# Batch 0's kv sum turned instead of direct, and three moves in the opening of an attention and MLP kernel

## The chip, the cores and the metric

The kernel runs on one NeuronCore of a Trainium2 chip. The metric is the device time of one execution in microseconds. The engines of the core are called by the names of the profile: PE is TensorE (matrix products; PEld is its loading of weights), DVE is VectorE, ACT is ScalarE, POOL is GpSimd, SP is SyncE, which here only issues transfers (DMA). Each engine works through its own queue in order, and engines wait for each other by semaphores.

## The reference, cut to what matters

A polynomial-sketch attention feeds a two-layer network with an exact GELU.

```python
batch, n_heads, seq, head_dim = (4, 4, 1088, 32); r = 8
def phi(x):
    a = einsum('rd,bhsd->bhsr', S1, x)
    b = einsum('rd,bhsd->bhsr', S2, x)
    return einsum('bhsi,bhsj->bhsij', a, b)          # flattened to 64 features
q_p, k_p = phi(q), phi(k)
kv  = einsum('bhsf,bhsd->bhfd', k_p, v)
z   = sum(k_p, axis=2)
num = einsum('bhsf,bhfd->bhsd', q_p, kv)
den = einsum('bhsf,bhf->bhs', q_p, z)[..., None] + 1e-6
x   = (num / den), heads side by side: (4352, 128)
out = gelu_exact(x @ w_in) @ w_out                    # w_in 128 x 2048, w_out 2048 x 128
```

q, k and v are float32. S1, S2, w_in and w_out arrive as float64, so the kernel rounds them to float32 itself.

## The kernel before, in words

**Chunks.** The 4352 tokens are worked in chunks of 512 tokens, two to a batch, and one last chunk that holds the 64 tokens left over of each batch. Chunk n is turned into features, divided, brought into the layout xT (128 features of x by 512 tokens) and then passed through the network: for each of 16 column tiles of w_in a hidden product (function `hidden`, line 683), GELU on ACT (690), and the product with w_out. For most of chunk time the second product runs in a scheme that takes seven block products where eight would be needed (`two_products`, 768); the first eight column tiles of chunks 0 and 1 use plain products (`project`, 819).

**The order of the work** is written out by hand. Lines 851 to 918 are the opening: the sketches, batch 0's keys and values, the features of chunk 0, the rounding of the first weights. After it a list of steps runs, one per chunk and column tile; other work is put at steps by `at(step, function)`. At the end of the program (1122 to 1128) every instruction is tied to the one before it on its engine, so each engine keeps the order of the text.

**Batch 0's kv.** Keys are transposed on PE (333), multiplied with the sketches (373), and turned to features by ACT and DVE or POOL (386 to 390). `kv_first` (411 to 418) then sums over tokens: 128 tokens at a time, the 64 features of a head are the stationary operand and 32 values with a one beside them (33 columns, which gives z as well) are the moving operand. Two heads use the two column halves of PE. `kv_first_rem` (420 to 424) adds the left-over tokens. The result stands as features by values, the layout which the numerators want, and one ACT copy (888) brings it from PSUM into `kz[0]`. Later batches do it the other way round: `kv_sum` (428) has v stationary and features moving, `take_kv` copies, and `turn_kv` turns the result on PE.

**Numerators and dividing.** `numerators_by_token` (635) multiplies chunk 0's expanded query features by `kz[0]`; `divide` (650 denominators, 651 reciprocals, 656 products) runs on DVE; `turn_half` (664, 665) transposes each half of 256 tokens and copies it to xT, half 0 by ACT and half 1 by DVE. `first_hidden` (698) starts the network on the halves.

**Expanding queries.** `expand_products` (534) makes both sketched factors of a chunk's query features, A in the first half of the columns and B in the second, in two pairs of PSUM banks; `expand_copy` (541, ACT) takes A to SBUF, `expand_multiply` (546, DVE) multiplies with B from PSUM. For chunk 1 the queries are transposed on PE by `query_turn(1)` (515, through 333), and the copy of that result is kept back and run at 895.

**Rounding weights.** `Rounding` splits the float64 words: ACT scales the low words (260), DVE cuts out exponent field (268) and mantissa field (273), ACT makes exponents (279), DVE adds the mantissa (287) and sign (292), and DVE or POOL forms the product (297). One piece of w_out gets its mantissa from ACT and POOL (284, 285). w_in has pieces of 256, 256, 512, 512 and 512 columns, w_out the same in rows.

**Loads.** SP issues them in one queue. The load of w_out's first two pieces is held back by two small POOL memsets (180) which stand behind POOL's product for w_in piece 0; every further load is queued behind them.

**Spread sketches.** `spread_sketches` (466 to 478) forms, with eight POOL instructions, copies of the sketches for the later batches. It is put at step 11; the matrix products that use it come first at 44.8 us.

## Time and profile before

| what | us |
|---|---|
| median of 3 runs | 264.18 (263.84 to 264.23) |
| the profiled execution | 264.42 |
| its span, first to last instruction | 262.6 |
| PE busy in the span | 257.3 (98%) |
| DVE busy | 151.3 (58%) |
| ACT busy | 116.7 (44%) |
| POOL busy | 163.8 (62%) |
| mean granted PE clock | 0.999 |

How to read a profile line: start and duration in us (or, in groups, the busy sum), the engine, the line of the kernel, the operation, what it writes and reads ("out<-in", partitions x elements), how many; in square brackets the idle time of the engine just before, and what ended it. In the chain of waits each row is a piece of the chain that ended last: start, length, engine, what it wrote, line. Matmuls are pipelined and their ends are modelled, and releasers are inferred from semaphores.

### The profile page before, as it was taken

What the parts mean: (1) busy time and instruction counts of PE and PEld (TensorE: products, weight loads), DVE (VectorE), ACT (ScalarE), POOL (GpSimd) and SP (SyncE); (2) the same over time, 40 slices, a digit from 0 to 9 for tenths busy, and PEclk for the clock granted to TensorE, in tenths of its full rate; (3) what the DMA queues carried; (4) which work ended last, traced back from release to release, by engine and by line L of the source; (5) the groups of instructions that cost most, each with busy time, mean ns of one, the idle gap of its engine ahead of it and who ended that gap; (6) DMA issues with size and microseconds to landing.
All of it is one profiled execution on the core that took longest, in us unless ns stands there. A gap on an engine that the chain in (4) does not pass through costs nothing.

```text
span 262.6 us, 5749 instructions
## 1 busy us (share of the span) xinstructions
PE 257.3 (98%) x2329; PEld 132.3 (50%) x2329; DVE 151.3 (58%) x307; ACT 116.7 (44%) x227; POOL 163.8 (62%) x173
## 2 busy tenths in 40 slices
PE   8999999999999999999999999999999999999994
PEld 6844444344454554444444455444444444445794
DVE  2885878969697996591267957450647042600240
ACT  3674777442635334543434334533362335433441
POOL 3403006899968676687767766867778676877200
PEclk9999999999999999999999999999999999999999
DMA  7479648730001101002000010011000100010020
GB/s 207 131 211 365 147 102 209 213 78 13 0 2 17 25 4 28 13 2 40 2 0 2 0 29 15 2 24 16 2 0 13 31 4 0 12 31 0 2 40 20
DMA packets 29530, 13.48 MB, mean 51 GB/s; under 512 B 21824, under 2 KB 27712, under 8 KB 29504
## 3 DMA queue, kind: packets, MB, share of 16 engines
q1 hardware_dynamic: 29472, 13.12, 20.2%
q8 instruction: 18, 0.29, 0.5%
q14 instruction: 8, 0.07, 0.1%
q10 hardware_dynamic: 32, 0.00, 0.0%
HBM read 10.88 MB, written 2.23 MB: 50 GB/s over the span
## 4 chain that ended last, share of the span: by engine, by line
PE 93%; DVE 3%; ACT 1%; issue 1%; POOL 1%; DVEq 0%
PE h_ps L683 43%; PE o_ps L768 33%; PE o_ps L819 5%; PE w_ps L816 3%; PE w_ps L617 2%; PE w_ps L428 1%; PE w_ps L849 1%; PE w_ps L568 1%; PE o_ps L417 1%; PE h_ps L333 1%; PE w_ps L935 1%; DVE q_pT L546 0%; PE w_ps L534 0%; DVE x_tok L656 0%; DVE w_out L297 0%
## 5 line engine op out<-in xcount | busy, mean ns | idle before, releaser
L683 PE MATMUL h_ps<-xT,w_in 128*64 128x512 f32 (+3 forms) x516 | 138.7, 577 | 0.0
L690 ACT ACTIVATE block<-h_ps 128x512 f32<-128x512 f32 (+1 forms) x128 | 73.0, 570 | 121.6 <-PE h_ps L683 115.1
L768 PE MATMUL o_ps<-block,w_out 128*64 128x256 f32 x224 | 57.8, 380 | 0.3 <-DVE sums L789 0.3
L683 PEld LDWEIGHTS h_ps<-xT,w_in 128*64 128x64 f32 (+1 forms) x516 | 42.0, 143 | 30.1 <-issue 11.4
L733 POOL TENSOR_TENSOR bits_low<-block 128x512 f32<-128x512 f32 x28 | 35.6, 1273 | 28.6 <-ACT block L690 28.6
L768 PEld LDWEIGHTS o_ps<-block,w_out 128*64 128x64 f32 x224 | 30.2, 137 | 38.8 <-issue 25.8
L734 POOL TENSOR_TENSOR bits_a<-block 128x512 f32<-128x512 f32 x28 | 35.7, 1277 | 14.0 <-ACT block L690 14.0
L735 POOL TENSOR_TENSOR bits_e<-bits_a,block 128x512 f32<-128x512 f32 x28 | 36.3, 1297 | 2.2
L736 POOL TENSOR_TENSOR bits_m<-block,bits_e 128x512 f32<-128x512 f32 x28 | 35.8, 1280 | 2.2
L784 DVE TENSOR_TENSOR sums<-o_ps,sums 64x512 f32<-64x512 f32 x8 | 5.5, 682 | 41.3 <-ACT sums L781 23.6
L768 PE MATMUL o_ps<-bits_low,small 128*64 128x256 f32 x112 | 29.2, 383 | 0.0
L768 PE MATMUL o_ps<-block,small 128*64 128x256 f32 x112 | 29.1, 383 | 0.0
L768 PE MATMUL o_ps<-bits_a,small 128*64 128x256 f32 x112 | 29.0, 382 | 0.0
L768 PE MATMUL o_ps<-bits_m,w_out 128*64 128x256 f32 x112 | 28.8, 380 | 0.0
L580 DVE STREAM_TRANSPOSE w_ps<-w_ps 128x512 f32<-128x512 f32 (+1 forms) x7 | 4.8, 691 | 38.5 <-PE w_ps L568 38.5
L768 PEld LDWEIGHTS o_ps<-block,small 128*64 128x64 f32 x112 | 14.7, 137 | 18.4 <-issue 10.0
L768 PE MATMUL o_ps<-bits_e,small 128*64 128x256 f32 x112 | 17.2, 385 | 0.0
L819 PE MATMUL o_ps<-g,w_out 128*128 128x512 f32 x32 | 16.4, 600 | 0.5 <-DVE w_out L297 0.5
L768 PEld LDWEIGHTS o_ps<-bits_m,w_out 128*64 128x64 f32 x112 | 15.4, 137 | 0.0
L768 PEld LDWEIGHTS o_ps<-bits_a,small 128*64 128x64 f32 x112 | 14.9, 137 | 0.0
L768 PEld LDWEIGHTS o_ps<-bits_low,small 128*64 128x64 f32 x112 | 14.7, 137 | 0.0
L690 ACT ACTIVATE g<-h_ps 128x512 f32<-128x512 f32 x16 | 9.5, 594 | 7.7 <-PE h_ps L683 7.1
(181 smaller groups left out, 297.2 us busy)
## 6 DMA issues: line engine op xcount, KB each, us to landing
out_dram<-oT SPq DMA_DIRECT2D x26, 64.0 KB, 2.2
block<-in_moe_w_in_dram SPq DMA_DIRECT2D x3, 512.0 KB, 7.1
block<-in_moe_w_out_dram SPq DMA_DIRECT2D x3, 512.0 KB, 13.0
k<-in_k_dram SPq DMA_DIRECT2D x12, 128.0 KB, 3.0
v<-in_v_dram SPq DMA_DIRECT2D x12, 128.0 KB, 3.3
q<-in_q_dram SPq DMA_DIRECT2D x24, 64.0 KB, 2.2
k<-in_k_dram SPq DMA_DIRECT2D x2, 256.0 KB, 2.8
q<-in_q_dram SPq DMA_DIRECT2D x2, 256.0 KB, 4.2
```

What stands on the lines that cost most here:

```text
L580: dve.transpose(out=tok, in_=ps[:, :, :H2])
L617: pe.matmul(banks[h * D:(h + 1) * D, s, i * N:(i + 1) * N], lhsT=(kz[b] if b else kz_first)[rows, h * D:(h + 1) * D], rhs=f[rows, h // 2, ...
L683: pe.matmul(ps[rows, :W], lhsT=w[:, rows], rhs=xT[n][:, :W], start=True, stop=True)
L690: act.activation(out=g_of[n, fi][:, :W], in_=ps[:, :W], func=ACT.Gelu)
L733: pool.tensor_sub(out=s[3], in0=a11, in1=a21)
L734: pool.tensor_add(out=s[1], in0=a21, in1=a22)
L735: pool.tensor_sub(out=s[2], in0=s[1], in1=a11)
L736: pool.tensor_sub(out=s[4], in0=a12, in1=s[2])
L768: pe.matmul(acc[n][bank][half * 64:(half + 1) * 64, col:col + HW], lhsT=fixed, rhs=moving, start=opens and e == 0 and name in "4715", stop ...
L784: dve.tensor_add(out=C[lo, 1], in0=a1[lo], in1=C[lo, 0])
L816: pe.matmul(o_of[n][i][:, :128], lhsT=g[:, i * 128:(i + 1) * 128], rhs=w_tile(w_out_sb, fi), start=first, stop=final)
L819: pe.matmul(o_of[n], lhsT=w_tile(w_out_sb, fi), rhs=g, start=first, stop=final)
```

## The change

- `kv_first` and `kv_first_rem` swap their operands: values with the one (33 columns) are stationary, the 64 features move. The sum stands as values by features in `kv_bank[:, :128]`.
- `take_kv_first` (new) copies it to SBUF with two ACT copies, one per head pair; `turn_kv_first` (new) turns it on PE with four products by the identity into `kv_bank[:, 128:256]`; the old copy to `kz[0]` reads from there. The turn is issued in the middle of `query_turn(1)`, between the second and the third transpose.
- The exponents of w_in piece 0 (279, ACT) move from ahead of that copy to behind it.
- Of chunk 0's two query multiplies (546, DVE), the second moves behind the field cuts of w_in piece 0.
- `expand_products` can do one half: chunk 1's A half stays where it was, `expand_copy(1, 0)` moves up behind the dividing, and the B half comes between the two `turn_half` calls.
- `spread_sketches` moves from step 11 into the opening, behind `widen_v_rem(0)`.

```diff
     def kv_first(ps, r, tokens=range(J)):
...
             for c in range(NP):
-                pe.matmul(ps[c * F:(c + 1) * F, r * 2 * D:r * 2 * D + C], lhsT=flat(k_p[0, r][:, t, c * 4 + ch * 2 + one]),
-                          rhs=v_aug[r][:, c, i, :C], start=(r == 0 and i == 0), stop=False, skip_group_check=True)
+                pe.matmul(ps[c * F:c * F + C, r * F:(r + 1) * F], lhsT=v_aug[r][:, c, i, :C],
+                          rhs=flat(k_p[0, r][:, t, c * 4 + ch * 2 + one]), start=(r == 0 and i == 0), stop=False,
+                          skip_group_check=True)
...
+    def take_kv_first(ps):
+        kv_T[0] = big.tile([128, 128], FP, name="kv_T_first")
+        for c in range(NP):
+            rows = slice(c * F, c * F + C)
+            act.copy(out=kv_T[0][rows], in_=ps[rows, :128])
+
+    def turn_kv_first(ps):
+        for c in range(NP):
+            rows = slice(c * F, c * F + C)
+            for r in range(2):
+                pe.matmul(ps[c * F:(c + 1) * F, r * F:r * F + C], lhsT=kv_T[0][rows, r * F:(r + 1) * F], rhs=ident[rows, rows],
+                          start=True, stop=True)
...
-    def expand_products(n):
+    def expand_products(n, parts=range(2)):
...
-        for i in range(2):
-            B_of[n, i] = work_banks()
-        for s in range(2):
+        if 0 in parts:
+            qp[n] = att.tile([128, 2, CW], FP, name="q_pT")
+            for i in range(2):
+                B_of[n, i] = work_banks()
+        for s in parts:
...
     widen_v_rem(0)
+    spread_sketches()
     expand_products(0)
-    for i in range(2):
-        query_features(0, i)
+    expand_copy(0, 0)
+    expand_copy(0, 1)
+    expand_multiply(0, 0)
...
     w_in[0].fields()
+    expand_multiply(0, 1)
+    take_kv_first(kv_bank)
+    late = []
+    query_turn(1, lambda **a: late.append(a), lambda: turn_kv_first(kv_bank[:, 128:256]))
+    kz_of, kv_of = (x.rearrange("f (r x) -> f r x", r=2)[:, :, :C] for x in (kz[0], kv_bank[:, 128:256]))
+    act.copy(out=kz_of, in_=kv_of)
     w_in[0].exponents()
-    late = []
-    query_turn(1, lambda **a: late.append(a))
-    kz_of, kv_of = (x.rearrange("f (r x) -> f r x", r=2)[:, :, :C] for x in (kz[0], kv_bank[:, :128]))
-    act.copy(out=kz_of, in_=kv_of)
...
-    expand_products(1)
+    expand_products(1, [0])
...
     w_in[1].mantissa_fields()
+    expand_copy(1, 0)
     turn_half(0, 0, hidden_bank(), by_act)
+    expand_products(1, [1])
     turn_half(0, 1, hidden_bank(), by_dve)
...
-    expand_copy(1, 0)
...
-    at(11, spread_sketches)
```

More of the change, by code (lines that the diff above doesn't have):

```diff
@@ L404, in key_features_rem @@
         dve.tensor_mul(**spread(k_p_rem[pair], a, ab[:, :, R:2 * R]))
-    k_s = {}
+    k_s, kv_T = {}, {}
     def flat(features):
@@ L422, in kv_first_rem @@
             for c in range(NP):
-                pe.matmul(ps[c * F:(c + 1) * F, r * 2 * D:r * 2 * D + C], lhsT=flat(k_p_rem[0][:, 2 * c + r]),
-                          rhs=v_rem_aug[0][:, 2 * c + r, :C], start=False, stop=True, skip_group_check=True)
+                pe.matmul(ps[c * F:c * F + C, r * F:(r + 1) * F], lhsT=v_rem_aug[0][:, 2 * c + r, :C],
+                          rhs=flat(k_p_rem[0][:, 2 * c + r]), start=False, stop=True, skip_group_check=True)
+    def take_kv_first(ps):
[9 more added lines that the diff above has]
+                          start=True, stop=True)
     def kv_product(ps, lhsT, features, h, part, start=False, stop=False):
@@ L447, in fold_z @@
         sketch_of_z(b, held["kv"][:, 0], F)
-    kv_T = {}
     def take_kv(b, ps):
@@ L509, with query_turn @@
     width = [CW] * NMAIN + [B // 2 * 128]
-    def query_turn(n, copy=by_act):
+    def query_turn(n, copy=by_act, midway=lambda: None):
         if n == 1:
-            turned = transposed(work_bank(), "qT", [q_sb[1][:, h].rearrange("p j d -> p (j d)") for h in range(H)], copy)
+            turned = transposed(work_bank(), "qT", [q_sb[1][:, h].rearrange("p j d -> p (j d)") for h in range(H)], copy,
+                                midway)
             qT[n] = turned.rearrange("p (h j t) -> p h j t", h=H, j=JC)
@@ L536, in expand_products @@
                               rhs=qT[n][rows, 2 * c:2 * c + 2].rearrange("p r j t -> p r (j t)"), start=True, stop=True)
-        qp[n] = att.tile([128, 2, CW], FP, name="q_pT")
     def expand_copy(n, i):
```

## The prediction

> **What bounds the kernel now.** I read the page first, its shares and its forty slices.

> ```profile
> span 262.6 us, 5749 instructions
> PE 257.3 (98%) x2329; PEld 132.3 (50%) x2329; DVE 151.3 (58%) x307; ACT 116.7 (44%) x227; POOL 163.8 (62%) x173
> PE   8999999999999999999999999999999999999994
> DVE  2885878969697996591267957450647042600240
> PEclk9999999999999999999999999999999999999999
> ```

> TensorE is full in nearly every slice at full clock, so work elsewhere counts only where TensorE waits. The reader should note DVE: 8, 8 and 5 in slices two to four, the opening (slices of 6.6 us). All edits lie there. Next I read the chain of waits in order of time, for the opening.

> ```profile
> 10.40 0.91 PE o_ps L417 x32
> 11.30 0.35 PE o_ps L423 x8
> 11.66 0.59 PE w_ps L333 x4
> 12.24 0.67 PE h_ps L635 x32
> 12.91 0.22 DVE den_tok L650 x2
> ...
> 14.93 0.42 PE h_ps L664 x2
> ...
> 22.34 0.21 POOL S_ab L476
> 22.55 0.05 issue
> 22.60 0.44 DVE w_out L297
> 23.04 0.14 issue
> 23.17 1.10 PE o_ps L819 x2
> ```

> Up to 12.9 us the chain is TensorE; from L650 at 12.9 to 23.2 it is almost wholly DVE (one pair of transposes, L664, comes between); after 23.17 it is TensorE with hardly a gap. So the time moves by what the start of L819 at 23.17 moves by. Two details of that stretch decide the case. First the timeline of ACT where the kv sum is handed over:

> ```profile
> 11.32 0.51 ACT L279 ACTIVATE bits_r<-bits_e,below 128x256 uint32<-128x256 uint32 x1 [0.36 <-DVE bits_e L268]
> 11.74 0.20 ACT L888 COPY kz<-o_ps 128x66 f32<-128x66 f32 x1
> ```

> Today the exponents of the first w_in piece (L279) are made while TensorE still sums, and one 0.20 us copy hands kv over. TensorE turns the second query chunk meanwhile (L333, 11.66 to 12.24), so the hand-over costs nothing. Then POOL and DVE just ahead of 23.17:

> ```profile
> 22.11 0.23 POOL L474 TENSOR_TENSOR S_abc<-sT,own_r 128x32 f32<-128x32 f32 x1
> 22.30 0.24 POOL L476 TENSOR_TENSOR S_ab<-sT,own_r 128x32 f32<-128x32 f32 x1
> 22.49 0.81 POOL L478 COPY S_abc<-S_abc 128x64 f32<-128x64 f32 x3
> 21.66 0.41 DVE L292 SCALAR_TENSOR_TENSOR bits_e<-small,bits_r 128x256 uint32<-128x256 uint32 x1
> 22.60 0.43 DVE L297 TENSOR_TENSOR w_out<-bits_m,bits_e 128x256 f32<-128x256 f32 x1 [0.53 <-POOL S_ab L476]
> ```

> L297 reads nothing of S_ab; what it needs from POOL (bits_m, L285) was written by 21.52. It sat idle 0.53 us and began when S_ab ended.

> [...] L297 has two SBUF inputs and waited out two POOL multiplies; then the second of the three L478 copies took 0.46 us and the others 0.23, while L297 ran. [...] No load stands alone in this trace; it does show pairs of L417 (64-column weights, 33 moving columns) 58 ns apart. [...] Between the last L423 and the first turn of L333 I read about 0.15 us.

> **The change part by part.**

> *Sketches earlier.* Eight POOL instructions (0.20, 0.16, 0.30, 0.23, 0.24, three copies of 0.23: about 1.7 us) leave 21.48 to 23.3 and go behind the widening of v_rem, which ends at 9.97. POOL's next work there is the product of L297 at 12.44, after 2.47 us of idleness, so they fit. [...] Gain: L292 ends at 22.07, so L297 goes 22.11 to 22.54 and L819 could start 0.14 later, at 22.68; TensorE's own L664 ends at 22.04 + 0.60 = 22.64, just ahead. **-0.49 us.** The memset of v_rem_aug now follows L285; it reads nothing. If the block is not what I take it for, the gain is 0.

> *kv with v stationary.* 72 TensorE instructions (L417 x64, L423 x8) keep their number; weights shrink from 64 to 33 columns and moving columns grow from 33 to 64. The nearest row is the later batches' sum, L428 (v stationary, 64 moving columns): its groups start 56 ns apart in the trace. So 36 pairs go from 58 to 56: **-0.07 us** (kv ends at 11.59). [...] I take -0.07, since L428 is the same form.

> *Copying kv out and turning it.* New between kv and kz: two ACT copies of 33x128, eight TensorE instructions, then the old copy of L888. A 128x128 copy out of PSUM takes 0.28 us (L335 at 9.72); two such ACT copies start 0.16 apart (L386, L389). With 0.05 us per hand-over (L399 end to L403 start is 0.04): copies 11.64 to 11.92 and to 12.09; turn from 11.98. All four instructions of a head pair use one tile, one after the other: 8 x 58 ns = 0.46, to 12.44; low end 8 x 29 = 0.23. The last result lands about 0.2 later (a MATMUL of L417 lasts 223 ns), so L888 starts at 12.65 and ends at 12.85; L635 starts at 12.91 instead of 12.17. The other two query transposes (L333) are queued behind the turn and fit into the 0.4 us while L888 waits and runs.

> *The exponents behind it.* L279 now stands behind L888 on ACT: 12.77 to 13.28. DVE's L292 waits for it, and behind L292 are queued L268 of w_in piece 1 and all of the dividing: L292 13.32 to 13.74, L268 to 13.94, L650 at 13.88 instead of 12.89: **+0.99 us**. Without that wait the numerators alone would give 12.91 + 0.72 = 13.63. The second expand multiply (0.64 us) moves behind L273 on DVE; it ends near 12.2 to 12.6, ahead of L292. Covered, else 0.64.

> *Chunk 1's expansion in halves.* Its 32 instructions (1.12 us at 13.24) become 2 x 0.56 around the first half's turn. The first half's xT is earlier, but the chain goes through the second: its x_tok is ready at 14.79 + 0.99 = 15.78, 15.92 with the hand-over[...]. **+0.05.** The earlier ACT copy of A (0.6 us) frees ACT where it was idle 1.16 us before L665. Nothing.

> *What starts later.* POOL's product of w_in piece 0, the two memsets behind it and SP's whole queue of loads start some 1.2 us later. w_out piece 1 landed at 18.72 and ACT reads it at 19.31: then 19.9 against 20.3. Covered, by 0.4 us.

> Sum: -0.49 + 0.99 + 0.05 = **+0.55 us** (the -0.07 is inside the 0.99). Span 262.6 becomes 263.15; the profiled execution, 264.42 (1.8 us around the span), becomes 264.97; it stood 0.24 above the median of 264.18, so 264.18 + 0.55 = **264.73**.

> **The rivals.**
> *Quick turn:* the eight instructions take 0.23 and hand-overs overlap. Everything from L888 on is 0.23 earlier: +0.32, 264.50. For it: some neighbours in L417 start 29 ns apart. Against: those use two tiles in turn, the new loop runs one head pair after the other.
> *The other side, absorption:* the idle times ahead of L650 (0.34) and of L665 (0.39) swallow 0.73 of the 0.99; 0.26 - 0.49 = -0.23, 263.95; with all of it absorbed, 263.69. It decides from 0.55 absorbed. Against: both idle times are hand-overs from TensorE that shift with the chain, and DVE is busy with hardly a gap from 15.4 to 20.3.
> *Late weights:* the loads behind the memsets become the bound. If w_out piece 1 lands more than 0.4 us later than shifted, ACT's L260 and DVE's L268 wait; SP's second issue already took 1.2 us. Price 0.3 to 0.8 on top: about 265.2.

> **How the numbers follow.** A measurement of this kernel tells 0.2% (0.53 us) from no change. Base case 0.54, own range 264.5 to 265.0, of which 0.42 lies above 264.71; quick turn 0.20 (same); late weights 0.14 (slower); absorption or an unseen gain 0.12, of which 0.10 faster by more than 0.2%. So slower 0.56, same 0.34, faster 0.10. To hold eight in ten, the range goes from 264.1, inside the quick turn's low side, to 265.3, the late weights.

> **What would show it.** L297 of w_out piece 1 starts right behind L292, without a wait on POOL; L888's copy starts near 12.65; DVE idles ahead of L292 until ACT's L279 ends near 13.3; L650 near 13.9; the start of the long L819 stretch near 23.7. I am wrong if kv ends well before 11.5, if L650 starts before 13.3, or if the 0.5 us idle ahead of L297 remains.

## The result and the profile after

The changed kernel took 264.87 us (median of 22 runs, 264.54 to 266.86), the kernel before 264.18 (median of 22 runs on the same chip). The ratio is 1.0032 with a 95% interval from 1.0018 to 1.0046: slower by 0.5 to 1.2 us. 264.73 had been forecast. The size was met, but of the three terms of the sum one was right, one too small, and one was not to be had where it was expected.

The page of the changed kernel, its head:

```profile
span 263.0 us, 5768 instructions
PE 257.5 (98%) x2337; PEld 131.9 (50%) x2337; DVE 150.2 (57%) x307; ACT 117.4 (45%) x229; POOL 163.4 (62%) x173
DVE  2786778969697996582177957460555042600240
```

PE has eight instructions more (the turn) and is as full as before (98%). DVE's second to fourth slices read 7, 8 and 6 where they read 8, 8 and 5. The next lines are the chain of waits of the changed kernel, for the opening; each row is start, length, engine, tile and line. Line 431 makes the two copies out of PSUM (the row shown is the second), 437 is the turn, 905 the copy into kz (888 before), 664 the denominators (650 before), 833 the plain product (819 before).

```profile
11.43 0.27 ACT kv_T_first L431
...
11.74 0.46 PE o_ps L437 x8
...
12.23 0.22 ACT kz L905
12.45 0.41 ACT bits_r L279
...
12.88 0.43 DVE bits_e L292
...
13.52 0.15 DVE den_tok L664 x2
...
22.84 0.46 issue
23.30 0.43 DVE w_out L297
...
23.87 1.10 PE o_ps L833 x2
```

Where the chain before ran from the kv sum through PE's query transposes to the denominators, it now runs through ACT twice, PE, ACT, ACT and DVE. At the other end the stop ahead of L297 is still there: 0.46 us of "issue", time in which the engine waited for nothing that the profile shows.

**A common zero.** Starts of two executions cannot be subtracted as they stand. In the profiled execution of the kernel before, PE was granted its full clock at 6.28 us; in that of the changed one at 4.80 us, so that the same four transposes (L333, at 5.22 and 5.11 us) took 1.11 us in the one and 0.65 in the other, and the first kv product came at 8.26 us instead of 8.70, though nothing ahead of it had changed for the better. In the eleven executions profiled here the full clock came anywhere from 3.89 to 6.32 us. From here on two kernels are compared by times counted from the first kv product (L417); the lines of a view keep the times of their own execution. This table, from the records of one execution of each kernel, carries the rest; the right column is what the end of the span moved by.

| kernel | first L417 at | denominators (L650) | DVE's copy of xT (L665) | second product of w_out (L297) | long stretch (L819) | end of span | against before |
|---|---|---|---|---|---|---|---|
| before | 8.70 | 4.19 | 6.68 | 13.90 | 14.47 | 253.92 | |
| changed | 8.26 | 5.17 | 7.83 | 15.04 | 15.62 | 254.74 | +0.82 |
| sketches alone | 8.32 | 4.15 | 6.63 | 13.85 | 14.42 | 253.54 | -0.38 |
| kv alone | 8.17 | 5.25 | 7.73 | 14.95 | 15.52 | 254.98 | +1.06 |
| halves alone | 8.23 | 4.19 | 7.06 | 14.28 | 14.85 | 254.29 | +0.37 |
| halves, copy late | 8.21 | 4.45 | 7.02 | 14.23 | 14.80 | 254.28 | +0.36 |
| three memsets on POOL | 8.06 | 4.19 | 6.68 | 13.48 | 14.07 | 253.19 | -0.73 |
| four more on DVE | 8.60 | 4.16 | 6.64 | 13.44 | 14.04 | 253.15 | -0.77 |
| changed, four more on DVE | 8.73 | 5.25 | 7.90 | 14.70 | 15.28 | 254.40 | +0.48 |
| one more on DVE | 8.00 | 4.54 | 7.01 | 13.82 | 14.41 | 253.53 | -0.39 |
| changed, exponents between | 8.68 | 5.07 | 7.93 | 15.15 | 15.72 | 254.84 | +0.92 |

The changed kernel's L664 stands 0.98 us later than L650 did: 0.99 was forecast. But the long stretch is 1.15 us later, not 0.55, and the end only 0.82. Two things are thus unexplained: 0.49 us that did not come in ahead of L297, and 0.3 us that came in somewhere behind 24 us.

### The profile page after: what moved, and what is told of

The parts are those of the page before. It is cut to its first block, busy times and chain, and to the rows that moved or that the text cites. A ratio compares the mean times of both kernels' runs of the same rounds, so it can differ in the third digit from the quotient of the medians.

```text
span 263.0 us, 5768 instructions
## 1 busy us (share of the span) xinstructions
PE 257.5 (98%) x2337; PEld 131.9 (50%) x2337; DVE 150.2 (57%) x307; ACT 117.4 (45%) x229; POOL 163.4 (62%) x173
## 2 busy tenths in 40 slices
PE   8999999999999999999999999999999999999994
DMA packets 29530, 13.48 MB, mean 51 GB/s; under 512 B 21824, under 2 KB 27712, under 8 KB 29504
## 4 chain that ended last, share of the span: by engine, by line
PE 96%; DVE 2%; ACT 1%; issue 0%; DVEq 0%
PE h_ps L697 45%; PE o_ps L782 33%; PE o_ps L833 5%; PE w_ps L830 3%; PE w_ps L631 1%; PE w_ps L442 1%; PE w_ps L863 1%; PE w_ps L582 1%; PE o_ps L417 1%; PE w_ps L549 1%; PE w_ps L954 1%; PE h_ps L333 1%; DVE x_tok L670 1%; PE w_ps L649 0%; PE w_ps L470 0%
## 5 line engine op out<-in xcount | busy, mean ns | idle before, releaser
L833 PE MATMUL o_ps<-g,w_out 128*128 128x512 f32 x32 | 16.4, 599 | 0.5 <-DVE w_out L297 0.5
```

Of the source, the lines that this page charges most:

```text
L833: pe.matmul(o_of[n], lhsT=w_tile(w_out_sb, fi), rhs=g, start=first, stop=final)
```

## The experiments

**One part at a time.** The kernel before, with one part of the change each.

The sketches alone:

```diff
     widen_v_rem(0)
+    spread_sketches()
     expand_products(0)
...
-    at(11, spread_sketches)
```

> The kernel before with only the eight POOL instructions of the spread sketches moved into the opening. Port theory (the prediction's: L297 of w_out piece 1 was blocked by POOL's multiplies): L297 starts within 0.05 us of the end of L292, the time falls by 0.49 us, ratio about 0.998. Place theory (DVE stops at the 64th instruction of its stream, whatever that is, since the 0.5 us idle ahead of L297 is still there in the changed kernel with POOL idle): L297 still starts about 0.5 us behind L292, ratio 1.000.

Measured: 263.74 us (16 runs), ratio 0.9988, interval 0.9977 to 1.0000. Its timeline, DVE and then POOL (start, busy time, engine, line, operation, and in brackets the idle time ahead and what ended it):

```profile
21.24 0.41 DVE L292 SCALAR_TENSOR_TENSOR bits_e<-small,bits_r 128x256 uint32<-128x256 uint32 x1
22.17 0.43 DVE L297 TENSOR_TENSOR w_out<-bits_m,bits_e 128x256 f32<-128x256 f32 x1 [0.52 <-DVE bits_e L292]
...
21.02 0.21 POOL L349 MEMSET v_rem_aug<- 128x128 f32 x1
```

POOL's last work ends at 21.23. From then on POOL does nothing, and L297 still sits idle for 0.52 us. So the two multiplies that stood beside the stop in the kernel before did not cause it. The long stretch starts 14.42 us behind the first L417, 0.05 earlier than before, and these 0.05 us stand already at the denominators (4.15 against 4.19), which four_more_on_dve below reaches at 4.16 with the sketches at their old place: they are no gain that the move can be shown to have made. Yet the end is 0.38 earlier: 0.33 us were won elsewhere.

The place was found by going along DVE and PE for idle time that nothing explains. The timeline of the kernel before, DVE and then PE, late in the program:

```profile
196.76 0.84 DVE L786 TENSOR_TENSOR sums<-o_ps,sums 64x256 f32<-64x256 f32 x2 [0.46 <-ACT block L690]
...
199.01 0.43 PE L768 MATMUL o_ps<-block,w_out 128*64 128x256 f32 x1 [0.28 <-DVE sums L789]
```

and the same line of DVE with the sketches moved:

```profile
195.99 0.85 DVE L786 TENSOR_TENSOR sums<-o_ps,sums 64x256 f32<-64x256 f32 x2
```

Before, DVE sits idle for 0.46 us ahead of L786, of which 0.28 lie behind the last thing that it waits for (ACT's L690 ends at 196.48), and PE, which is waiting for the chain of sums, stands still for 0.28 us at 199.01. With the sketches moved L786 follows the instruction before it without idle time worth a bracket, and PE has no such gap. No instruction near it was touched. What differs is a count. In DVE's recorded stream, its waits on semaphores counted with its instructions, L297 is the 64th record in both kernels, with a wait as the 63rd. L786 is the 320th in the kernel before, again behind a wait; with the sketches moved DVE needs two waits less further up (they stood as the 119th and the 193rd record), L786 becomes the 318th, and the 320th is L787 with no wait ahead of it. The distance is 256.

The page of the kernel before lists the transfers that bring instructions:

```profile
q14 instruction: 8, 0.07, 0.1%
```

Eight packets during the span and 0.07 MB; the records give 8192 bytes to each. One such packet starts at 197.42, 0.66 us behind the start of L786. The distance and this packet made the **place theory**, at this point a guess of the author's: DVE stops at certain places of its instruction stream, whatever instruction stands there, and the stop is seen only where a wait stands just ahead.

The kv part alone (the kv hunks of the diff, the exponents behind kz, the second multiply moved, the expansion left whole and the sketches at step 11):

```diff
     w_in[0].fields()
-    w_in[0].exponents()
+    expand_multiply(0, 1)
+    take_kv_first(kv_bank)
     late = []
-    query_turn(1, lambda **a: late.append(a))
-    kz_of, kv_of = (... for x in (kz[0], kv_bank[:, :128]))
+    query_turn(1, lambda **a: late.append(a), lambda: turn_kv_first(kv_bank[:, 128:256]))
+    kz_of, kv_of = (... for x in (kz[0], kv_bank[:, 128:256]))
     act.copy(out=kz_of, in_=kv_of)
+    w_in[0].exponents()
```

> The kernel before with only the kv part of the change: v and ones stationary, copied out and turned, the exponents of w_in piece 0 behind the copy to kz, the second query multiply behind the field cuts. By the prediction's sum L650 (the first denominators) starts 0.99 us later counted from the first kv product, and the time rises by 0.99 us, ratio 1.0037. If the delay is taken up downstream (the rival called absorption), it rises by 0.3 us or less, ratio 1.001.

Measured: 265.30 us (6 runs), ratio 1.0039, interval 1.0026 to 1.0052, or 1.03 us by the ratio. Its chain of waits:

```profile
12.22 0.22 ACT kz L904
12.44 0.41 ACT bits_r L279
...
23.69 1.10 PE o_ps L833 x2
```

Counted from the first L417, the copy into kz stands within 0.1 us of its time in the changed kernel (4.05 against 3.97) and the exponents follow it as there, though neither sketches nor halves were touched. The long stretch is 1.05 us later than before (15.52 against 14.47) and the end by 1.06. This part alone more than explains the slowdown.

The split expansion alone:

```diff
-    expand_products(1)
+    expand_products(1, [0])
     for banks, tokens in zip(nd, parts):
         divide(0, banks, tokens, by_head_pair=True)
     w_in[1].mantissa_fields()
+    expand_copy(1, 0)
     turn_half(0, 0, hidden_bank(), by_act)
+    expand_products(1, [1])
     turn_half(0, 1, hidden_bank(), by_dve)
     for half in range(2):
         first_hidden(half, range(1))
-    expand_copy(1, 0)
```

> The kernel before with only chunk 1's expansion made in two halves. By the prediction's sum plus 0.00 to 0.09 us, ratio 1.000; the transposes of the second half start at most 0.1 us later behind their x_tok. If the halves are what costs the time instead of the kv part, ratio 1.002 or more.

Measured: 264.36 us (22 runs), ratio 1.0016, interval 1.0006 to 1.0027, and the end 0.37 us later. That is far above the 0.05 forecast. Its timeline, PE and DVE:

```profile
14.18 0.69 PE L536 MATMUL w_ps<-qT,Srep 32*64 32x256 f32 x16 [0.22 <-ACT A_sb L542]
15.28 0.42 DVE L666 COPY xT<-h_ps 128x256 f32<-128x256 f32 x1 [0.78 <-PE h_ps L665]
```

against DVE's copy in the kernel before:

```profile
15.38 0.42 DVE L665 COPY xT<-h_ps 128x256 f32<-128x256 f32 x1 [0.39 <-PE h_ps L664]
```

The second half's 16 products write other columns of the tile that ACT's early copy is reading (13.55 to 14.13), and they wait for that copy: 0.22 us of PE, and DVE idles 0.78 us for its xT instead of 0.39.

To see whether that wait is the cause, the copy went back to its old place behind both halves and the split was kept:

```diff
     w_in[1].mantissa_fields()
-    expand_copy(1, 0)
     turn_half(0, 0, hidden_bank(), by_act)
     expand_products(1, [1])
     turn_half(0, 1, hidden_bank(), by_dve)
     for half in range(2):
         first_hidden(half, range(1))
+    expand_copy(1, 0)
```

> The kernel before with the split expansion alone, as in halves_alone, but ACT's copy of A for chunk 1 left at its old place, behind both halves. If halves_alone lost its time because the second half's products wait for ACT's copy of the first (0.22 us on TensorE, L536 behind L542), that wait goes: L666 on DVE starts about 6.83 us behind the first L417 instead of 7.06 (before: 6.68), and the time falls from 1.0016 to about 1.0007; what is left, 0.15 us, is the split's own cost on TensorE. Rival: the split and its changes of tiling are the whole cost, and the copy only filled a gap: 7.06 stays, ratio about 1.0014. If the copy at its early place had been of use further on (for the multiplies behind L297), the ratio is above 1.0016.

Measured: 264.31 us (14 runs), ratio 1.0008, interval 0.9996 to 1.0020, as expected, though it overlaps with that of halves_alone. In the timeline DVE waits 0.49 us for its xT:

```profile
15.22 0.42 DVE L666 COPY xT<-h_ps 128x256 f32<-128x256 f32 x1 [0.49 <-PE h_ps L665]
```

From the denominators to the copy of xT it is 2.57 us, against 2.87 in halves_alone (7.06 - 4.19) and 2.49 before (6.68 - 4.19): 0.30 of the 0.38 are gone with the wait, 0.08 belong to the split. The copy did not start at the expected 6.83, since in this one execution PE stalled within the numerators and L651 came 0.26 us later than in the others; why isn't known. So by this trace the wait is the larger part of the cost, and by the times alone it stays unproven.

**The place theory.** First, three DVE memsets of the very beginning went to POOL, so that everything behind them is three places earlier in DVE's stream:

```diff
-    dve.memset(ones, 1.0)
+    pool.memset(ones, 1.0)
...
-        dve.memset(t[:, :, :, D:C], 1.0)
+        pool.memset(t[:, :, :, D:C], 1.0)
```

> The kernel before with the three small DVE memsets of lines 237 and 241 issued by POOL instead, so that every later DVE instruction stands three places earlier in DVE's stream; the spread sketches stay where they were. Place theory: the 0.5 us stop falls three instructions later, on the mantissa cut L273 of w_in piece 2, behind which DVE waits 2.2 us for ACT anyway; L297 starts right behind L292 and the time falls by about 0.49 us, ratio 0.998. Port theory: POOL's multiplies still run at 22 us, L297 waits as before, ratio 1.000.

Measured: 263.41 us (5 runs), ratio 0.9966, interval 0.9954 to 0.9979: faster than both kernels. Its timeline, DVE and POOL:

```profile
21.02 0.41 DVE L292 SCALAR_TENSOR_TENSOR bits_e<-small,bits_r 128x256 uint32<-128x256 uint32 x1
21.54 0.45 DVE L297 TENSOR_TENSOR w_out<-bits_m,bits_e 128x256 f32<-128x256 f32 x1
...
21.48 0.23 POOL L474 TENSOR_TENSOR S_abc<-sT,own_r 128x32 f32<-128x32 f32 x1
21.67 0.41 POOL L476 TENSOR_TENSOR S_ab<-sT,own_r 128x32 f32<-128x32 f32 x1
...
99.05 0.23 DVE L483 TENSOR_TENSOR z_s<-w_ps,sT 128x64 f32<-128x64 f32 x1 [0.23 <-issue]
```

L292 ends at 21.43 and L297 starts 0.10 us later, beside POOL's multiplies as ever; now it is POOL's L476 that is stretched, 0.41 us instead of 0.24. The stop at 196.8 is gone as well. The 64th record is now an L273 with no wait just ahead, and it runs without a stop. One stop is new: 0.23 us at 99.05, put down to "issue". It stands at the 192nd record (half way between the 64th and the 320th), two records and 0.45 us behind the end of a wait; the instruction between covers the rest.

But this edit also took work from DVE. So the next adds work instead: four tiny memsets more at the head of DVE's stream, nothing else.

```diff
     dve.memset(ones, 1.0)
+    pads = big.tile([128, 4], FP, name="pads")
+    for i in range(4):
+        dve.memset(pads[:, i:i + 1], 0.0)
```

> The kernel before with four small memsets more at the head of DVE's stream: more work, nothing taken away. Place theory (the stop ahead of L297 belongs to the place, 64th in DVE's recorded stream, when a wait on a semaphore stands just ahead of it): L297 becomes the 68th instruction and starts about 0.05 us behind its wait instead of 0.47, L819 starts 0.4 to 0.5 us earlier counted from the first L417, and the stop of 0.28 us at the 320th instruction goes too, since a transpose with no wait ahead of it stands there now: ratio about 0.997. Port theory (POOL's two multiplies hold L297 back): the idle time ahead of L297 stays near 0.5 us, ratio 1.000. If only fewer memsets on DVE helped, the ratio is 1.000 or a little above.

Measured: 263.53 us (8 runs), ratio 0.9972, interval 0.9962 to 0.9982. Four useless instructions made the kernel 0.7 us faster. Its timeline, DVE (lines are three higher), and from the chain of waits the start of the long stretch:

```profile
21.52 0.41 DVE L295 SCALAR_TENSOR_TENSOR bits_e<-small,bits_r 128x256 uint32<-128x256 uint32 x1
22.04 0.45 DVE L300 TENSOR_TENSOR w_out<-bits_m,bits_e 128x256 f32<-128x256 f32 x1
...
22.64 1.10 PE o_ps L822 x2
```

The product (L300 here) starts 0.10 us behind the end of the sign step (21.94) where it had started 0.53 behind. No stop is left at 196.8, and from 14.80 us on the chain is PE's up to the long stretch. The place theory had asked for just that; its rival, that POOL's multiplies hold L297 back, for no change at all.

With one memset more the wait itself is the 64th record and L297 the 65th:

```diff
+    pads = big.tile([128, 1], FP, name="pads")
+    dve.memset(pads, 0.0)
```

> The kernel before with one small memset more on DVE. Now the wait ahead of L297 is the 64th instruction and L297 the 65th. If the stop comes at the 64th instruction whatever it is, the wait itself starts 0.4 us late or so; if it needs a wait just ahead of the 64th, or if it comes only where the two stand on either side of the boundary, there is no stop and L819 starts 0.4 to 0.5 us earlier, as with four more.

One execution took 263.30 us. Its timeline of DVE:

```profile
12.09 0.53 DVE L270 TENSOR_SCALAR bits_e<-small 128x256 uint32<-128x256 uint32 x1 [0.44 <-DMA small<-in_moe_w_in_dram]
...
21.82 0.44 DVE L299 TENSOR_TENSOR w_out<-bits_m,bits_e 128x256 f32<-128x256 f32 x1
```

The step ahead of it ends at 21.71: no stop, neither at the wait nor behind it. So a wait at that place is not enough: a stop there was seen only with the wait as the 63rd record. (That the denominators came late in this execution, at 4.54, is another matter: with the clock granted as early as 3.89 us the opening ran ahead of a load of w_in, and L270 waited 0.44 us for it.)

Last, the same four memsets in the changed kernel:

```diff
     dve.memset(ones, 1.0)
+    pads = big.tile([128, 4], FP, name="pads")
+    for i in range(4):
+        dve.memset(pads[:, i:i + 1], 0.0)
```

> The changed kernel with four small memsets more on DVE. Place theory: the 0.46 us ahead of L297 go, L833 starts 0.4 to 0.5 us earlier counted from the first L417 (about 15.1 us behind it instead of 15.61); the 320th instruction waits for TensorE there anyway, so nothing more is won: ratio 1.0032 - 0.0018 = about 1.0014. Port theory: the same as the changed kernel, 1.0032.

Measured: 264.61 us (17 runs), ratio 1.0014, interval 1.0003 to 1.0025. The row of the long stretch in its chain of waits:

```profile
24.00 1.10 PE o_ps L836 x2
```

The stop is gone and PE now sets the start of the long stretch, 15.28 us behind the first L417. The gain in the opening is 0.34 us, not 0.46 as expected, since PE's own work ends there. Between the two kernels without stops the difference is 1.0014 / 0.9972 = 1.0042, some 1.1 us, give or take 0.4 by the two intervals: that is what the change costs once neither has the stop ahead of L297, and more than the 0.69 us between the medians.

**What the 0.98 us consist of.** In the changed kernel ACT is idle while PE turns kv. There L279 was put:

```diff
     take_kv_first(kv_bank)
+    w_in[0].exponents()
...
     act.copy(out=kz_of, in_=kv_of)
-    w_in[0].exponents()
```

> The changed kernel with L279 of the first w_in piece between the copies out of PSUM and the copy of kz, while TensorE turns kv. My theory of the 0.99 us: part of it is that L279 stands behind kz on ACT. Then L292 starts near 12.25 instead of 12.88, L664 waits for the numerators alone (kz copy, 0.22 + L649, 0.67) and starts about 4.95 us behind the first L417 instead of 5.17: 0.2 us won, ratio about 1.0024; some 0.75 us of the shift stay, which are the copies, the turn and the hand-overs. Rival (the place of L279 doesn't matter because the numerators set the start already): L664 stays at 5.17, ratio 1.0032. If kv form and turn cost nothing of themselves and all is the queue: 0.9 us won, ratio about 0.9998.

Measured: 265.33 us (7 runs), ratio 1.0037, interval 1.0024 to 1.0050: nothing won. Its timeline, ACT, DVE and PE:

```profile
12.22 0.51 ACT L279 ACTIVATE bits_r<-bits_e,below 128x256 uint32<-128x256 uint32 x1
12.75 0.22 ACT L906 COPY kz<-o_ps 128x66 f32<-128x66 f32 x1
...
13.74 0.23 DVE L664 TENSOR_SCALAR den_tok<-h_ps 128x4 f32<-128x4 f32 x2 [0.35 <-PE h_ps L649]
...
15.51 0.69 PE L549 MATMUL w_ps<-qT,Srep 32*64 32x256 f32 x16 [0.22 <-ACT A_sb L555]
```

DVE's denominators do start earlier, 5.07 us behind the first L417 instead of 5.17, and wait for the numerators now, as expected. Only half of the expected 0.2 us shows because in this execution the kv sum itself ended later, 2.95 us behind the first L417 against 2.87 in that of the changed kernel. Why isn't known; but it was so in kv_alone (2.95) and in the changed kernel with four more memsets (2.94) too, where L279 stands behind kz. Against the latter the denominators are 0.18 us earlier (5.07 against 5.25), near what was expected. L279, which ends at 12.73, holds the copy of kz back by some 0.02 us.

Yet DVE's xT does not come earlier: 7.93, against 7.90 there and 7.83 in the changed kernel. The second half's products now wait 0.22 us for ACT's copy of A, as in halves_alone. So two paths of nearly one length lead to the second half of xT: through DVE's denominators, and through PE's expansion and ACT's copy of A. To shorten the first alone is worth nothing while the second stands; what L279's place on ACT costs without the halves was not tried.

## Why the prediction was right and where it was wrong

**"Copying kv out and turning it" and "the exponents behind it" (+0.99): right in the path, and lucky in the size.** L664 moved by 0.98 (by 1.06 in kv_alone). Counted from the first L417, the forecast had the kz copy at 3.95, L292 at 4.62 and the denominators at 5.18; measured were 3.97, 4.62 and 5.17. Inside it two sizes were off and cancelled, which was luck. The two ACT copies ran one behind the other (0.27 apart, not 0.16) and the turn waited for the second, not the first: it began 0.2 us later than forecast. The turn itself was shorter than forecast. The timeline of PE in the changed kernel has it as one row:

```profile
11.74 0.43 PE L437 MATMUL o_ps<-ident,kv_T_first 33*64 33x33 f32 x8 [0.25 <-ACT kv_T_first L431]
```

All eight take 0.43 us from the first start to the last end, and the last one alone takes 0.22 of it by its record, so they start within 0.21 us: about 30 ns apart, the pace of the rival called quick turn, though the loop runs one head pair after the other, which had been the argument against it. The forecast had 0.46 us for the eight and 0.2 more for the landing of the last. So half of that rival came true; its gain of 0.2 us was used up by the hand-over of the copies, which it had expected to overlap. Absorption did not happen: the idle times moved along, and kv_alone gave the whole 1.05 us at the long stretch.

**"kv with v stationary" (-0.07): right within what can be read.** The last 32 products of L417 take 1.06 us instead of 1.08. From the first L417 to the end of the kv sum it took 2.96 us before, 2.87 changed, 2.95 in kv_alone: two executions of the new form differ by more than the term.

**"Sketches earlier" (-0.49): wrong, and the failed step is "It sat idle 0.53 us and began when S_ab ended".** That was a coincidence of two ends within 0.05 us, and it was made into a cause, which the trace had not shown. spread_alone removed the multiplies and the 0.52 us stayed; memsets_on_pool kept the multiplies and the idle time went. That the idle time stays had been named beforehand as a sign of being wrong, and it stayed. In memsets_on_pool L297, with two SBUF inputs, started at 21.54 beside a POOL multiply recorded from 21.48 to 21.71 and took 0.45 us instead of 0.43, so it did not wait for that multiply to end (spans on POOL are rough, which leaves some room). four_more_on_dve shows the same: 22.04, beside a multiply from 21.98 to 22.22, and again 0.45 us. The one that took longer was POOL's next multiply, which came second: 0.41 us in the first of these runs and 0.42 in the other, instead of 0.24. In the opening the move won nothing that can be told from the scatter of 0.05 us. What it cost there was covered: in the changed kernel, beside POOL's sketches, DVE's L268 took 0.40 us instead of 0.29 and L273 0.32 instead of 0.28, 0.15 us together, and behind them DVE waited 0.84 us for ACT's L279 in any case.

**What was not in the sum at all: -0.33 us behind the long stretch.** From the start of the long stretch to the end of the span the table gives 239.44 to 239.48 us for the four kernels that have the stop ahead of L786 (before, kv alone and both with the halves alone), and 239.11 to 239.12 for the seven others. PE's standstill at 199.01 is 0.28 us of the difference. The move of the sketches won it by taking two waits from DVE's stream. It is the main part of the 0.38 us that spread_alone won, and the reason why the changed kernel lost 0.82 us at its end but 1.15 at the long stretch.

**"Chunk 1's expansion in halves" (+0.05): mis-sized, and the failed step is "The earlier ACT copy of A frees ACT ... Nothing".** The copy reads a tile that the second half still has to write, so it put a wait of 0.22 us on PE: alone, +0.37 us at the end. The 0.05 itself was the author's estimate; halves_copy_late, without that wait, has 0.08 for the split. In company with the kv part the second half is held up by the first half's transposes anyway (L678 ends at 14.97, ACT's copy at 14.94), and the halves cost 0.10 us there: 15.62 against 15.52 in kv_alone. (At DVE's xT, where no stop is in the way, it is 0.10 us for the changed kernel and 0.17 for the one with four more memsets: 7.83 and 7.90 against 7.73.)

**"What starts later": right.** No engine waits for a transfer between 14 and 24 us in the changed kernel, so the late weights did not come.

The sum was -0.49 + 0.99 + 0.05 = +0.55. Measured, by the part runs and the table: nothing to -0.05 for the sketches in the opening, +1.05 for kv, +0.10 to 0.17 for the halves, -0.33 for the stop that went, together about +0.8, against +0.82 in the profiled executions, +0.85 by the ratio and +0.69 between the medians. The forecast of 264.73 lay close by luck: a gain that was misread in the opening was replaced by a smaller one 170 us later that nobody had looked for.

## What to carry to other kernels

When an engine sits idle and something else ends at that moment, ask first whether the idle time is a wait at all: count the instruction's place in its stream, look for the same stop elsewhere at a fixed distance (256 records here), and move the place by a few harmless instructions before rearranging real work. Count times from a common event when the clock is granted at different moments (3.89 to 6.32 us here), and look at the end of the span as well as at the stage that was changed. A sum that must be copied out of PSUM, turned and copied again costs two hand-overs more on the path (here, with the work between them and what was queued behind, 1.0 us). And splitting work into halves saved nothing here, where the first half's reader and the second half's writer share a tile.

## What the runs showed of the hardware that had not been expected

What DVE does at these places was not shown. The packets that bring instructions stand near two of the three. In the four kernels with the stop at the 320th record one starts 0.66 to 0.70 us behind the start of L786; in memsets_on_pool, with its stop at the 192nd, one starts at 99.75, 0.69 us behind that record, where the ten other kernels have theirs between 94.0 and 96.0. But none was under way during a stop, and behind the 64th record of the seven kernels that stop there the next one comes only 3.3 to 4.7 us later. So the cause of the stop stays open.
